# The second MLP's first product as seven products of halves, in units of 768 tokens, with w_out's parts read from DRAM

## The chip, the cores and the metric

The kernel runs on one core of a Trainium2 chip. The metric is the device time of one execution in microseconds (us). Before the change it is 1026.53 us, the median of three runs (1025.58 to 1028.79). All traces are profiles of one execution; times inside a trace count from the start of its span.

## The reference

Attention with a decay and a causal mask (4 sequences of 576 tokens, 8 heads of 64) gives x with 2304 tokens of 512 features. Two MLPs follow, one on the other's output:

```python
h = x @ w_in            # 512 -> 2048
r = np.maximum(h, 0.0)
x = (r * r) @ w_out     # 2048 -> 512
```

Everything is float32. The change is in the second of the two MLPs.

## The kernel before

A float32 matrix product is made of three products on the matrix engine (PE): each operand is cut into a high part, rounded to a shorter format that PE takes in one pass (fp32r), and a low part, the rest; high x high, high x low and low x high are added up in PSUM. A high part is a cast on ScalarE (ACT), a low part a subtraction on VectorE (DVE) or GpSimd (POOL).

The attention runs beside the first MLP (mlp_a), which goes over nine groups of 256 tokens. Sixteen tiles of the pool wp hold the first MLP's weights, one for each block of 128 hidden features: w_in's high and low part, then w_out's. The first MLP's output goes to y_d in DRAM. When its last group has used a weight tile for the last time, that tile takes the second MLP's weights of the same block. Those weights come from DRAM as 64-bit words; DVE takes three operations on 512 columns for each 512 KB (decode, L796 to L800), for 32 such words in all, w_in's and w_out's sixteen each.

The second MLP (mlp_b) goes over groups of 512 tokens: four, and a last one of 256. For each group the tokens are loaded from y_d and split (L983, L990, L993), alternately into a tile on the right (ysr) and one on the left (ysl) of SBUF. For each of 16 blocks PE makes the first product, 12 matmuls (4 blocks of the 512 inputs by 3 parts) into one of two banks hp (L841); ACT takes its positive part out of PSUM (L850), DVE multiplies that with the bank again (L853, the square), ACT casts it (L863) and POOL makes the low part (L866). The second product takes 12 matmuls of 512 columns, 3 for each 128 tokens, into four banks that hold the group's output (bk, L1015). After 16 blocks ACT and DVE evacuate them (L1025, L1027) and SP stores them.

The order of all instructions on an engine is fixed when the program is built: a planner plays the program through with its own costs and priorities (the first numbers in op(...)), and each engine then works through its list in order, waiting for semaphores. A list that waits holds up everything behind it. An operation given to either of two engines is placed by the planner. SP's list holds all DMAs.

## Time and profile before

| | us |
|---|---|
| median of the runs | 1026.53 |
| the profiled execution itself | 1022.93 |
| its span, first to last instruction | 1021.1 |
| PE busy | 995.2 |
| VectorE busy | 526.8 |
| ScalarE busy | 490.2 |
| GpSimd busy | 294.6 |
| DMA moved | 98.35 MB |

PE's granted clock is 90% or more of full speed in all but the second of the forty slices of the span, where the attention starts, and full in every stretch looked at from 100 us on. Busy times say how much an engine has to do. What an engine waits for, and whether that matters, is read from the chain of waits, which goes back from the last instruction to what released each step.

### The profile page before, as it was taken

How to read it: one execution, taken by the hardware profiler on the slowest of the kernel's cores; microseconds unless marked ns; L12 is line 12 of the kernel's file. 1: busy time of each engine (PE TensorE's matmuls, PEld its weight loads, DVE VectorE, ACT ScalarE, POOL GpSimd, SP SyncE). 2: the span in 40 equal slices, each digit the busy share in tenths (PEclk: the TensorE clock that was granted, in tenths of full speed). 3: DMA queues.
4: the chain of work that ended last, by engine and by line, in shares of the span. 5: the costliest groups of instructions: out<-in, count | busy, mean ns of one | idle time of the engine just before them, and what ended most of it. 6: DMA issues, size and time to landing. Idle time of an engine off the chain costs nothing.

```text
span 1021.1 us, 17203 instructions
## 1 busy us (share of the span) xinstructions
PE 995.2 (97%) x6637; PEld 865.6 (85%) x6637; DVE 526.8 (52%) x1241; ACT 490.2 (48%) x1001; POOL 294.6 (29%) x286
## 2 busy tenths in 40 slices
PE   5999999999999999999999999999999999999998
PEld 3888898887888898888999998888888888888897
DVE  7998666676677767677377698412112211211111
ACT  3766667777677777676222364322223222222222
POOL 2111143433434434333232222222222222222222
PEclk9799999999999999999999999999999999999999
DMA  9776246665665666566456344101000100000010
GB/s 248 228 215 182 80 95 127 133 133 122 130 135 123 133 134 129 119 120 127 104 162 179 107 132 155 44 1 62 21 1 1 62 1 1 11 32 1 1 42 21
DMA packets 164418, 98.35 MB, mean 96 GB/s; under 512 B 133936, under 2 KB 146992, under 8 KB 164208
## 3 DMA queue, kind: packets, MB, share of 16 engines
q1 hardware_dynamic: 164336, 97.25, 38.3%
q8 instruction: 52, 0.85, 0.3%
q14 instruction: 30, 0.25, 0.1%
HBM read 59.91 MB, written 10.03 MB: 68 GB/s over the span
## 4 chain that ended last, share of the span: by engine, by line
PE 84%; DVE 6%; DMA 6%; ACT 1%; issue 1%; SPq 1%; POOL 0%; DVEq 0%; ACTq 0%; POOLq 0%
PE hp L841 35%; PE bk L1015 19%; PE yp L916 16%; PE bk L732 7%; PE bk L692 4%; DMA sa<-in_w_dram 3%; DMA st<-in_w_dram 2%; PE bk L565 1%; PE bk L605 1%; DVE tmp L798 1%; DVE tmp L800 1%; PE bk L607 1%; DMA qk<-aug_d 0%; DVE wb L798 0%; DVE wb L800 0%
## 5 line engine op out<-in xcount | busy, mean ns | idle before, releaser
L866 POOL TENSOR_TENSOR gt<-sq,gt 128x512 fp32r<-128x512 f32 (+1 forms) x152 | 191.7, 1261 | 514.1 <-ACT gt L863 488.1
L853 DVE SCALAR_TENSOR_TENSOR sq<-hp,sq 128x512 f32<-128x512 f32 (+1 forms) x144 | 95.1, 661 | 332.8 <-ACT sq L850 332.5
L916 PE MATMUL yp<-gt,w 128*128 128x256 f32 x1728 | 232.5, 284 | 2.2 <-POOL gt L866 1.5
L841 PE MATMUL hp<-xk,w 128*128 128x256 f32 x1728 | 229.8, 285 | 0.0
L916 PEld LDWEIGHTS yp<-gt,w 128*128 128x128 f32 x1728 | 219.5, 191 | 4.4 <-POOL gt L866 2.1
L841 PEld LDWEIGHTS hp<-xk,w 128*128 128x128 f32 x1728 | 217.9, 192 | 0.5
L1015 PE MATMUL bk<-w,gt 128*128 128x512 f32 x864 | 209.8, 391 | 0.0
L850 ACT ACTIVATE sq<-hp 128x512 f32<-128x512 f32 (+1 forms) x152 | 87.4, 575 | 234.6 <-PE hp L841 201.5
L1015 PEld LDWEIGHTS bk<-w,gt 128*128 128x128 f32 x864 | 161.0, 188 | 34.3
L863 ACT CAST gt<-sq 128x512 fp32r<-128x512 f32 (+1 forms) x152 | 90.8, 598 | 158.1 <-PE bk L1015 109.8
L841 PE MATMUL hp<-ysr,w 128*128 128x512 f32 (+1 forms) x576 | 120.6, 358 | 0.0
L841 PEld LDWEIGHTS hp<-ysr,w 128*128 128x128 f32 x576 | 97.2, 188 | 18.4
L404 ACT ACTIVATE pp<-pp,stat 128x448 f32<-128x448 f32 (+1 forms) x128 | 78.3, 612 | 38.9 <-DVE stat L396 27.4
L841 PE MATMUL hp<-ysl,w 128*128 128x512 f32 x384 | 91.9, 389 | 0.0
L426 DVE SCALAR_TENSOR_TENSOR ph<-pp,stat,ph 128x320 f16<-128x320 f32 (+2 forms) x96 | 71.8, 751 | 27.8 <-ACT ph L419 26.7
L841 PEld LDWEIGHTS hp<-ysl,w 128*128 128x128 f32 x384 | 72.1, 188 | 14.9
L396 DVE CUSTOM_DVE_ANT_0 pp<-bk,mask 128x448 f32<-128x448 f32 (+1 forms) x128 | 59.3, 473 | 39.5 <-PE bk L692 38.8
L732 PE MATMUL bk<-pt,vv 64*128 64x64 f16 (+7 forms) x672 | 77.7, 253 | 0.0
L732 PEld LDWEIGHTS <-vv 128*128 128x128 bf16 (+3 forms) x672 | 37.0, 101 | 38.8 <-issue 24.9
L419 ACT ACTIVATE ph<-pp,stat 128x320 f16<-128x320 f32 (+2 forms) x96 | 63.6, 664 | 10.7 <-DVE stat L413 8.6
L435 POOL TENSOR_TENSOR vv<-vv 128x320 f32<-128x320 f32 x64 | 51.8, 809 | 55.7 <-DMA vv<-in_v_dram 51.1
L647 POOL TENSOR_TENSOR qk<-raw,qk 64x384 fp32r<-64x384 f32 x32 | 33.4, 1043 | 92.2 <-ACT qk L638 90.3
(132 smaller groups left out, 781.7 us busy)
## 6 DMA issues: line engine op xcount, KB each, us to landing
st<-in_w_dram SPq DMA_DIRECT2D x20, 512.0 KB
raw<-in_qk_dram SPq DMA_DIRECT2D x32, 288.0 KB
sa<-in_w_dram SPq DMA_DIRECT2D x18, 512.0 KB
X<-in_w_dram SPq DMA_DIRECT2D x14, 512.0 KB
vv<-in_v_dram SPq DMA_DIRECT2D x32, 160.0 KB
out_dram<-st SPq DMA_DIRECT2D x18, 256.0 KB
yf<-y_d SPq DMA_DIRECT2D x4, 1024.0 KB
raw<-in_w_dram SPq DMA_DIRECT2D x6, 512.0 KB
```

Of the source, the lines that this page charges most:

```text
L396: nc.vector.tensor_tensor_reduce(out=x[:rows, c0:c0 + wd], in0=src, in1=msk, scale=-0.125, scalar=3.0e38 if first else nmax[:rows, 5:6], o ...
L404: nc.scalar.activation(out=x, in_=x, func=AF.Exp, scale=-1.0, bias=nmax[:rows, t:t + 1], accum_out=ssum[:rows, t:t + 1])
L419: nc.scalar.activation(out=a, in_=x, func=AF.Copy, scale=r)
L426: nc.vector.scalar_tensor_tensor(out=flat[:rows, z:z + wd], in0=x, scalar=r, in1=flat[:rows, 128 * blk:128 * blk + wd], op0=ALU.mult, op1= ...
L732: nc.tensor.matmul(dst.rearrange("p (n c) -> p n c", n=rh.shape[1]), lhsT=lt, rhs=rh, start=(i == 0), stop=(i == len(todo) - 1), skip_grou ...
L841: nc.tensor.matmul(ps, lhsT=lt, rhs=rh, start=(k_ == 0 and c == 0), stop=(k_ == KD - 1 and c == 2))
L850: nc.scalar.activation(out=sq()[:, :c], in_=ps()[:, :c], func=AF.Relu)
L853: nc.vector.scalar_tensor_tensor(out=sq()[:, :c], in0=ps()[:, :c], scalar=0.0, in1=sq()[:, :c], op0=ALU.max, op1=ALU.mult)
L863: nc.scalar.copy(out=gt[0]()[:, :c], in_=sq()[:, :c])
L866: eng.tensor_tensor(out=gt[1]()[:, :c], in0=sq()[:, :c], in1=f32(gt[0]()[:, :c]), op=ALU.subtract)
L916: nc.tensor.matmul(yp[d // 2]()[:, d % 2], lhsT=lt, rhs=rh, start=(i == 0 and c == 0 and d % 2 == 0), stop=(i == NF - 1 and c == 2), skip_ ...
L1015: nc.tensor.matmul(ob[c](), lhsT=lt[:, cs], rhs=rh, start=(i == 0 and z == 0), stop=(i == NF - 1 and z == 2))
```

## The change

The second MLP works on units of 768 tokens, three in all. Its first product multiplies w_in, a matrix of 512 by 2048, with the tokens, in pairs of blocks: block p and block p+8 of the hidden features, by two halves of the 512 inputs, by two halves of 384 tokens. Such a product of two 2 x 2 matrices of blocks is made by seven products of blocks instead of eight. Their left operands are l11, l12, l22 and four sums s1 to s4 of w_in's blocks, their right operands r11, r21, r22 and four sums t1 to t4 of the tokens' quarters; each is split into its high and low part. A product takes 6 matmuls of 384 columns (2 blocks of 128 inputs by 3 parts). The seven results are combined after the product: ACT copies the first out of PSUM, and DVE makes seven sums, each of a bank and a tile in SBUF, of which four are the pair's hidden features (in r). The square then multiplies r with itself, 768 columns at a time, and the cast and the low part are 768 columns wide too.

The left operands of pairs 1 to 5 (p from 0 to 4) go into nine of the sixteen weight tiles as the first MLP frees them, the right operands of a unit into six; the last tile holds two buffers for w_out. The operands of pairs 6 to 8 are prepared during the first unit, in tiles (far) that are opened when all else is prepared. w_out's high and low parts are made once and stored in DRAM (wo_d); each step reads two blocks of them back, 512 KB each, in all units. The second product has six banks, one for each 128 tokens of a unit, and its matmuls are planned between the products of the next pair.

In the diff, tiles move too (sq, gt and xk go to a pool that is closed when the first MLP is done). Decoding a word takes the same three operations as before.

```diff
+    TU, TH, NP = 3 * GA, 3 * GA // 2, NF // 2
+    NU, NC = NT // TU, TU // 128
...
+    def unit_runs(u):
+        if u < 2:
+            return [(TH * x, (2 * u + x) * S, TH) for x in range(2)]
+        return [(TH // 2 * b, b * S + TH, TH // 2) for b in range(B)]
...
+    LEFT = ("l22", "l11", "l12", "s1", "s2", "s3", "s4")
+    RIGHT = ("r11", "t2", "r21", "t3", "t1", "t4", "r22")
+    ORDER = tuple(zip(("l11", "s2", "l12", "s3", "s1", "l22", "s4"), RIGHT))
+    wo_d = dram.tile([NF, 128, 2, 512], F32R, name="wo_d")
+    NEAR = 5
...
+    SUM, STAGEX, LWX = Pool([xf[:, 0:1024]]), Pool([xf[:, 1024:2048], xf[:, 2048:3072]]), Pool([xf[:, 3072:4096]])
+    UT = Pool([None] * 3, True)
+    RB, GTB = Pool([None] * 2, True), Pool([None] * 3, True)
+    RW = Pool([None] * 2, True)
...
+    SLOTS = ("s0", "l0", "s1", "l1", "s2", "l2", "s3", "s4", "l3", "y0", "y1", "y2", "y3", "y4", "y5", "ring")
...
+    def w_out_parts(i, prio, deps):
+        word, part = Buf(WORD), Buf(PART)
+        o = words(i, 1, STAGE, word, prio, deps, [word])
+        o = op("ACT", act(512), lambda: nc.scalar.copy(out=part()[:, 0], in_=word()), prio, [o], [word, part])
+        o = either_vp(512, lambda e: e.tensor_tensor(out=part()[:, 1], in0=word(), in1=f32(part()[:, 0]), op=ALU.subtract), prio, [o], [word, part])
+        return op("SP", P.COPY[0], lambda: nc.sync.dma_start(out=f32(wo_d[i]), in_=f32(part())), prio, [o], [part], data=1.46)
...
+    def w_in_forms(p, stage, lw, prio, deps, late, free):
+        l, sm = Buf(lw), Buf(SUM)
+        os_ = [words(i, 0, stage, lambda h=h: l()[:, h * 512:h * 512 + 512], prio, deps, [l]) for h, i in enumerate((p + NP, p))]
...
+        e = None
+        for f, a, b, how in (("s1", "l21", "l22", ALU.add), ("s2", "s1", "l11", ALU.subtract), ("s3", "l11", "l21", ALU.subtract), ("s4", "l12", "s2", ALU.subtract)):
+            e = either_vp(256, lambda eng, f=f, a=a, b=b, how=how: eng.tensor_tensor(out=x(f), in0=x(a), in1=x(b), op=how),
+                          prio, os_ + [e] + late, [l, sm])
...
+            n = 256 * (k - j)
+            dep = [slot_op[SLOTS[at[LEFT[j]]]]] if p < NEAR else [free]
+            h = op("ACT", act(n), lambda parts=parts: parts(0), prio, (os_ if j < 3 else [e]) + dep, uses)
+            got += [h, either_vp(n, lambda eng, parts=parts: parts(1, eng), prio, [h], uses)]
+            j = k
+        return got
...
+        def total(f, a, b, deps):
+            return either_vp(TU, lambda eng: eng.tensor_tensor(out=src(f), in0=src(a), in1=src(b), op=ALU.subtract), 40.0, deps)
+        done = {"r11": split("r11", ld)}
...
+    def first_products(q, u, p, ys):
+        t0, t1 = Buf(UT), Buf(UT)
+        r0, r1 = Buf(RB), Buf(RB)
+        g1, g0 = Buf(GTB), Buf(GTB)
+        h0, h1 = slice(0, TH), slice(TH, TU)
+        prods, prev = [], {}
+        e0 = EL + 1000 + q
...
+        def add(o, a, b):
+            return lambda: nc.vector.tensor_tensor(out=o(), in0=a()[:, 0:TH], in1=b(), op=ALU.add)
...
+        steps = (
+            [("copy", t0, None, [t0])],
+            [("u2", t1, t0, [t0, t1])],
+            [("c11", cols(r0, h0), t0, [t0, r0])],
+            [("u3", t0, t1, [t0, t1])],
+            [("c22", cols(r1, h1), t0, [t0, r1]), ("u4", t1, t1, [t1])],
+            [("c21", cols(r1, h0), t0, [t0, r1])],
+            [("c12", cols(r0, h1), t1, [t1, r0])],
+        )
+        after = dict(u2=["copy"], c11=["copy"], u3=["u2", "c11"], c22=["u3"], u4=["u3"], c21=["u3"], c12=["u4"])
+        done = {}
+        for s_, (lf, rf) in enumerate(ORDER):
+            ps = Buf(HP)
+            def prod(ps=ps, lf=lf, s_=s_):
+                for k_ in range(2):
+                    (wh, wl), (xh, xl) = form(p, lf, k_), y_form(s_, k_)
+                    for c, (lt, rh) in enumerate(((wh, xh), (wh, xl), (wl, xh))):
+                        nc.tensor.matmul(ps()[:, 0:TH], lhsT=lt, rhs=rh, start=(k_ == 0 and c == 0), stop=(k_ == 1 and c == 2))
+            m = op("PE", 6 * mmr(TH), prod, MLP + 10000 + 100 * q + 10 * s_, forms_of[p] + ys[s_], [ps])
+            prods.append(m)
+            for name, o, b, uses in steps[s_]:
+                if b is None:
+                    done[name] = op("ACT", act(TH, True), lambda o=o, ps=ps: nc.scalar.copy(out=o(), in_=ps()[:, 0:TH]), e0, [m], [ps] + uses)
+                else:
+                    done[name] = op("DVE", dve(TH), add(o, ps, b), e0, [m] + [done[x] for x in after[name]] + (late_ops if name[0] == "c" else []), [ps] + uses)
+        ready = []
+        for r, g, deps in ((r1, g1, [done["c21"], done["c22"]]), (r0, g0, [done["c11"], done["c12"]])):
+            o = op("DVE", dvs(TU), lambda r=r: nc.vector.scalar_tensor_tensor(out=r(), in0=r(), scalar=0.0, in1=r(), op0=ALU.max, op1=ALU.mult), e0, deps, [r])
+            h = op("ACT", act(TU), lambda r=r, g=g: nc.scalar.copy(out=g()[:, 0], in_=r()), e0, [o], [r, g])
+            l = either_vp(TU, lambda e, r=r, g=g: e.tensor_tensor(out=g()[:, 1], in0=r(), in1=f32(g()[:, 0]), op=ALU.subtract), e0, [h], [r, g])
+            ready.append((g, l))
+        return prods, ready
+    def second_products(q, u, p, ready, ob, last):
...
+        for x, ((g, lo), i) in enumerate(zip(ready, (p + NP, p))):
+            rw = Buf(RW)
+            ld = op("SP", P.COPY[0], lambda rw=rw, i=i: nc.sync.dma_start(out=f32(rw()), in_=f32(wo_d[i])), EL + 1000 + q, [out_ready[i], slot_op["ring"]], [rw], data=1.46)
+            for c in range(NC):
+                def m2(c=c, rw=rw, g=g, x=x):
+                    for z, (a, b) in enumerate(((0, 0), (0, 1), (1, 0))):
+                        nc.tensor.matmul(bank(ob[c]), lhsT=g()[:, a, c * 128:(c + 1) * 128], rhs=rw()[:, b], start=(p == 0 and x == 0 and z == 0),
+                                         stop=(p == NP - 1 and x == 1 and z == 2))
+                last[c] = op("PE", 3 * mmr(DM), m2, MLP + 10000 + 100 * (q + 1) + 10 * (n // 2 + 1) + 5, [lo, ld, last[c]], [g, rw, ob[c]])
+                n += 1
+    def store_unit(u, last, ob, deps):
...
-        opened_words = op("POOL", 0.01, open_words, -1.0e7, all_att)
...
-        opened_first = op("POOL", 0.01, open_first, -1.0e7, first_words)
-        opened_second = op("POOL", 0.01, open_second, -1.0e7, second_words)
-        dep = [opened_first]
-        for g, (t0, n) in enumerate(GB):
-            dep = [mlp_b(g, dep + [y for x in range(NGA) if any(t0 < s + k and s < t0 + n for _, s, k in runs(x * GA, (x + 1) * GA)) for y in y_stored[x]])]
...
+        last_a = [m2_of[0, NGA - 1, i] for i in range(NF)]
+        slots(last_a)
+        opened_prep = op("POOL", 0.0, open_prep, -1.0e7, all_att)
+        prep, near = [], []
+        for p in range(NP):
+            if p < NEAR:
+                forms_of[p] = w_in_forms(p, STAGE, LW, 9000.0 + 100.0 * p, [opened_prep], x_read, None)
+                prep += forms_of[p]
+            for i in (p + NP, p):
+                out_ready[i] = w_out_parts(i, 9050.0 + 100.0 * p, [opened_prep])
+                prep.append(out_ready[i])
+        opened_far = op("POOL", 0.0, open_far, -1.0e7, prep)
+        late_ops.append(op("POOL", 0.0, open_late, -1.0e7, last_a + x_read))
+        gone, taken, far = [[] for _ in RIGHT], [], []
+        waiting, sums = None, []
+        for u in range(NU):
+            stored = [y for x in range(NGA) if any(t < s + k and s < t + n for _, s, k in runs(x * GA, (x + 1) * GA) for _, t, n in unit_runs(u))
+                      for y in y_stored[x]]
+            ys, taken = inputs(u, x_read + [opened_prep] + stored + sums + far, gone, taken)
+            sums = [y for x in ys for y in x] + taken
+            if u == 0:
+                for p in range(NEAR, NP):
+                    forms_of[p] = w_in_forms(p, STAGEX, LWX, 9000.0 + 100.0 * p, sums, [], opened_far)
+                    far += forms_of[p]
+            ob, last = accumulators(), [None] * NC
+            for p in range(NP):
+                prods, ready = first_products(u * NP + p, u, p, ys)
+                second_products(u * NP + p, u, p, ready, ob, last)
+            gone = [[x] for x in prods]
+            store_unit(u, last, ob, far)
```

The change leaves the order of every engine as it was up to the end of the attention. PE's order in the middle of a unit, before (hp is the first product's bank, bk the output's banks, w the weights, gt the squared hidden features; x12 is twelve matmuls):

```order
L841 MATMUL hp0_85<-ysr_6645,w_6587 128x512 x12
L1015 MATMUL bk0_81<-w_6554,gt0_75 128x512 x2
L1015 MATMUL bk0_81<-w_6554,gt1_76 128x512
L1015 MATMUL bk1_82<-w_6554,gt0_75 128x512 x2
L1015 MATMUL bk1_82<-w_6554,gt1_76 128x512
L1015 MATMUL bk2_83<-w_6554,gt0_75 128x512 x2
L1015 MATMUL bk2_83<-w_6554,gt1_76 128x512
L1015 MATMUL bk3_84<-w_6554,gt0_75 128x512 x2
L1015 MATMUL bk3_84<-w_6554,gt1_76 128x512
L841 MATMUL hp1_86<-ysr_6645,w_6620 128x512 x12
```

and after (yp are two more output banks, g the squared features of 768 tokens; both operands of the first product and w_out's buffer stand in tiles w):

```order
L1212 MATMUL hp1_89<-w_6827,w_6696 128x384 x6
L1212 MATMUL hp0_88<-w_6871,w_6729 128x384 x6
L1238 MATMUL bk0_84<-w_6985,g1_6991 128x512 x3
L1238 MATMUL bk1_85<-w_6985,g1_6991 128x512 x3
L1212 MATMUL hp1_89<-w_6886,w_6696 128x384 x6
L1238 MATMUL bk2_86<-w_6985,g1_6991 128x512 x3
L1238 MATMUL bk3_87<-w_6985,g1_6991 128x512 x3
L1212 MATMUL hp0_88<-w_6926,w_6729 128x384 x6
L1238 MATMUL yp0_90<-w_6985,g1_6991 128x512 x3
L1238 MATMUL yp1_91<-w_6985,g1_6991 128x512 x3
L1212 MATMUL hp1_89<-w_6937,w_6729 128x384 x6
L1238 MATMUL bk0_84<-w_6985,g2_6992 128x512 x3
```

One product of 12 matmuls and all groups of the second took turns before; now two products of 6 stand at the start of each step and then single ones with two groups between them.

DVE's order while the second MLP's weights are decoded, before (sq is the square, sa the two tiles that loads arrive in, wb a decoded word; DMAHW is a wait for a DMA):

```order
L853 SCALAR_TENSOR_TENSOR sq_74<-hp_86,sq_74 128x512 [waits Activation_49]
L796 TENSOR_SCALAR wb_5706<-sa_5709 128x512 [waits DMAHW4_49]
L798 SCALAR_TENSOR_TENSOR wb_5706<-sa_5709,wb_5706 128x512 [waits DVE_49]
L796 TENSOR_SCALAR wb_5707<-sa_5710 128x512 [waits DMAHW5_49]
L800 SCALAR_TENSOR_TENSOR wb_5706<-sa_5709,wb_5706 128x512 [waits DVE_49]
L798 SCALAR_TENSOR_TENSOR wb_5707<-sa_5710,wb_5707 128x512 [waits DVE_49]
L800 SCALAR_TENSOR_TENSOR wb_5707<-sa_5710,wb_5707 128x512 [waits DVE_49]
L853 SCALAR_TENSOR_TENSOR sq_73<-hp_85,sq_73 128x512 [waits Activation_49]
L853 SCALAR_TENSOR_TENSOR sq_74<-hp_86,sq_74 128x512 [waits Activation_49]
L796 TENSOR_SCALAR X<-X 128x512 [waits DMAHW6_49,Pool_49]
```

and after, at the start of the first unit (hp, the sums' bank; st_82, st_83 and u their tiles in SBUF; stage, where a load arrives, word and X, which take a decoded one):

```order
L1052 SCALAR_TENSOR_TENSOR word_5707<-stage_5705,word_5707 128x512
L1048 TENSOR_SCALAR word_5706<-stage_5704 128x512 [waits DMAHW6_49]
L1189 TENSOR_TENSOR r_6994<-hp_88,st_82 128x384 [waits DVE_49,PE_49]
L1189 TENSOR_TENSOR st_83<-hp_88,st_83 128x384
L1189 TENSOR_TENSOR r_6994<-hp_89,st_82 128x384 [waits PE_49]
L1223 SCALAR_TENSOR_TENSOR r_6994<-r_6994 128x768 [waits DVE_49]
L1189 TENSOR_TENSOR r_6993<-hp_88,st_83 128x384 [waits PE_49]
L1050 SCALAR_TENSOR_TENSOR word_5706<-stage_5704,word_5706 128x512
L1225 TENSOR_TENSOR g_6990<-r_6994,g_6990 128x768 [waits Activation_49]
L1223 SCALAR_TENSOR_TENSOR r_6993<-r_6993 128x768 [waits DVE_49]
L1189 TENSOR_TENSOR st_82<-hp_88,u 128x384 [waits PE_49,Activation_49]
L1189 TENSOR_TENSOR r_6994<-hp_89,u 128x384 [waits DVE_49,PE_49]
```

Decode operations that wait for a DMA now stand between the sums that free the two banks hp.

DVE's order at the end of the first unit's fifth step, after the change only (far is pair 6's operands):

```order
L1223 SCALAR_TENSOR_TENSOR r_6993<-r_6993 128x768 [waits DVE_49]
L1189 TENSOR_TENSOR r_6994<-hp_89,st_83 128x384 [waits PE_49]
L1223 SCALAR_TENSOR_TENSOR r_6994<-r_6994 128x768 [waits DVE_49]
L1101 TENSOR_TENSOR far_7363<-X,far_7363 128x3x256 [waits DMAHW6_49,Activation_49]
L1189 TENSOR_TENSOR st_82<-hp_89,u 128x384 [waits PE_49,Activation_49]
L1189 TENSOR_TENSOR r_6993<-hp_88,u 128x384 [waits PE_49,Pool_49]
L1048 TENSOR_SCALAR X<-X 128x512 [waits DMAHW0_49,DVE_49]
L1048 TENSOR_SCALAR X<-X 128x512
```

The low part of pair 6's first operands stands between the fifth step's last square and the sixth step's first sums.

## Rows read from the trace of the kernel before

**Rows 1.** Page: PE's busy time, share of the span, instructions

```profile
PE 995.2 (97%) x6637; PEld 865.6 (85%) x6637; DVE 526.8 (52%) x1241; ACT 490.2 (48%) x1001; POOL 294.6 (29%) x286
```

**Rows 2.** Chain of waits, end of the first MLP to the end: start, us, what

```profile
614.25 1.44 PE yp L916 x12
615.69 2.81 PE hp L841 x12
618.50 1.43 PE yp L916 x12
...
639.45 2.81 PE hp L841 x12
642.26 2.76 PE bk L1015 x12
...
736.25 2.72 PE hp L841 x12
738.97 2.72 PE bk L1015 x12
...
1010.63 6.82 PE bk L1015 x30
1017.45 0.02 issue
1017.48 0.69 DVE st L1027
```

**Rows 3.** Busy times by stretch: us, PE, PEld, DVE, ACT, POOL, PE clock, DMA

```profile
500.00:628.00 128.00, 126.02 (x1013) 123.83 (x1012) 96.99 (x141) 46.84 (x82) 32.26 (x24) 1.00 0.46 141
560.00:570.00 10.00, 8.25 (x67) 7.85 (x66) 4.35 (x7) 2.84 (x5) 3.30 (x3) 1.00 0.30 105
```

**Rows 4.** Groups by shape, POOL and ACT: count, busy us, mean ns, idle before

```profile
L866 POOL TENSOR_TENSOR gt<-sq,gt 128x512 fp32r<-128x512 f32 x136 | 179.8, 1322 | 481.8 <-ACT gt L863 455.8 <-issue 14.4 <-PE hp L841 8.4
...
L863 ACT CAST gt<-sq 128x512 fp32r<-128x512 f32 x136 | 84.3, 620 | 142.1 <-PE bk L1015 93.8 <-DVE sq L853 46.4 <-PE yp L916 0.8
L850 ACT ACTIVATE sq<-hp 128x512 f32<-128x512 f32 x136 | 81.3, 598 | 219.7 <-PE hp L841 201.5 <-POOL gt L866 17.5
...
L866 POOL TENSOR_TENSOR gt<-sq,gt 128x256 fp32r<-128x256 f32 x16 | 11.8, 738 | 32.4 <-ACT gt L863 32.4
...
L863 ACT CAST gt<-sq 128x256 fp32r<-128x256 f32 x16 | 6.5, 407 | 16.0 <-PE bk L1015 16.0
...
L850 ACT ACTIVATE sq<-hp 128x256 f32<-128x256 f32 x16 | 6.2, 385 | 14.9 <-POOL gt L866 14.9
```

**Rows 5.** Line of the square: min, median and max ns, first and last start

```profile
L853 DVE SCALAR_TENSOR_TENSOR sq<-hp,sq x144: 424/692/694, 126.2 to 1013.5; 128x512 f32<-128x512 f32 x128, 128x256 f32<-128x256 f32 x16
```

**Rows 6.** Timeline, PE and ACT near 799 us: start, us, engine, line

```profile
798.88 1.32 PE L1015 MATMUL bk<-w,gt 128*128 128x512 f32 x5
799.13 0.60 ACT L850 ACTIVATE sq<-hp 128x512 f32<-128x512 f32 x1 [2.48 <-PE hp L841]
```

**Rows 7.** Timeline, POOL and DVE near 551 us

```profile
551.30 1.29 POOL L866 TENSOR_TENSOR gt<-sq,gt 128x512 fp32r<-128x512 f32 x1 [3.14 <-ACT gt L863]
...
551.35 1.78 DVE L798 SCALAR_TENSOR_TENSOR wb<-sa,wb 128x512 uint32<-128x512 uint32 x1
```

**Rows 8.** Line of a decode operation: min, median and max ns, first and last start

```profile
L798 DVE SCALAR_TENSOR_TENSOR wb<-sa,wb x10: 678/692/1785, 531.9 to 563.9; 128x512 uint32<-128x512 uint32 x10
```

**Rows 9.** Waits of DVE, 500 to 630 us: total us, times, longest

```profile
DVE wb L796 <- DMA sa<-in_w_dram: 10.6, 8, 3.6
...
DVE wa L796 <- DMA sa<-in_w_dram: 4.0, 4, 1.8
```

**Rows 10.** Timeline, SP's load of the last 256 tokens, 512 KB

```profile
791.78 0.53 SPq L983 DMA_DIRECT2D yf<-y_d  x1
```

**Rows 11.** Busy times by stretch behind that load, DMA share and GB/s last

```profile
791.50:793.50 2.00, 2.00 (x10) 1.62 (x9) 0.25 (x1) 0.00 (x0) 1.41 (x1) 1.00 0.17 21
793.50:795.50 2.00, 2.00 (x10) 1.62 (x9) 0.69 (x1) 0.60 (x1) 0.00 (x0) 1.00 0.76 239
```

More of the change, by code (lines that the diff above doesn't have):

```diff
@@ L942, in mlp_a @@
         y_stored[g] = outs
-    GB = [(t0, min(512, NT - t0)) for t0 in range(0, NT, 512)]
-    YF, YS = Pool([None]), Pool([None, None])
-    NWA, NWB = 8, 11
-    SA, WA, WB = Pool([None] * 2), Pool([None] * NWA), Pool([None] * NWB)
-    right, left = ExitStack(), ExitStack()
-    def place(pools, n, shape, dt, name, pl):
-        for x, y in zip(pools.free, tiles(pl, n, shape, dt, name)):
+    TU, TH, NP = 3 * GA, 3 * GA // 2, NF // 2
+    NU, NC = NT // TU, TU // 128
+    assert (B, S) == (4, 3 * TH // 2)
@@ L955, in place, with open_prep @@
             assert x[2] is None
             x[2] = y
[L958 removed]
+    def open_prep():
         att_stack.close()
[L960 to L970 removed]
@@ new lines, in open_prep @@
+        keep = ctx.enter_context(tc.tile_pool(name="keep", bufs=1, side="left", reuse_waits="tile"))
+        two_t.append(keep.tile([128, 2, TH], F32, name="t2"))
+        place(UT, [x[:, 512:512 + TH] for x in st_] + [keep.tile([128, TH], F32, name="u")])
+        pl = prep_stack.enter_context(tc.tile_pool(name="prep", bufs=1, side="left", reuse_waits="tile"))
+        place(STAGE, tiles(pl, 2, [128, 1024], F32, "stage"))
+        place(WORD, tiles(pl, 2, [128, 512], F32, "word"))
+        place(PART, tiles(pl, 2, [128, 2, 512], F32R, "part"))
@@ new lines, in open_prep, with open_far, open_late @@
+        place(LW, tiles(pl, NEAR, [128, 1024], F32, "lw"))
+    def open_far():
+        prep_stack.close()
+        pl = ctx.enter_context(tc.tile_pool(name="far", bufs=1, side="left", reuse_waits="tile"))
+        for p, x in zip(range(NEAR, NP), tiles(pl, NP - NEAR, [128, 7, 512], F32R, "far")):
+            for j, f in enumerate(LEFT):
+                WB[p, f] = (x, j)
+    def open_late():
+        mid_stack.close()
+        pl = ctx.enter_context(tc.tile_pool(name="late", bufs=1, side="right", reuse_waits="tile"))
+        place(GTB, tiles(pl, 3, [128, 2, TU], F32R, "g"))
+        place(RB, tiles(pl, 2, [128, TU], F32, "r"))
@@ L1198, in attention_then_two_squared_relu_mlps @@
-        for i in range(NF):
-            stage, words, deps = places(2 * i)
-            before = len(decoded)
-            got = weights(1, i, 9000.0 + 100.0 * i, 9000.0 + 100.0 * i, deps, [m2_of[0, NGA - 1, i]], stage, words)
-            if words is WA:
-                first_words += got
-            if words is WB:
-                second_words += got
-            if stage is SA:
-                first_words += decoded[before:]
-        opened_first = op("POOL", 0.01, open_first, -1.0e7, first_words)
```

216 lines of the change are left out of this document (144 added, 72 removed).

## Prediction

> **What bounds the kernel now.** First the busy times [rows 1]: the matrix engine PE works 995.2 us of 1021.1, so a change pays only by what it takes off PE's own time, less the waits it brings. Then the chain of waits [rows 2]: from 614.25 us to the end it is nothing but PE, so the second MLP has no wait in it. It starts at 615.69 us and its last product ends at 1017.45: 401.76 us, in which three runs of the first MLP still stand (the row at 618.50 and two like it, 4.3 us together). The second MLP costs PE 397.5 us. The same rows give the price of a product: 12 with 256 columns take 1.44 us, 120.0 ns each; 12 with 512 columns take 2.72 us (226.7 ns) to 2.81 us (234 ns) for the first product and 2.72 to 2.76 us (226.7 to 230 ns) for the second. The two levels alternate with the token group; I can't say why, and keep both. Last, the stretch in which the second MLP's weights are decoded, 500 to 628 us [rows 3]: PE is busy 126.0 of 128.0 us, and 1.75 of the lost 2.0 us fall between 560 and 570 us.
>
> **What the change takes from PE.** A step of the new code is a pair of feature tiles with a unit of 768 tokens: 7 products of 6 matmuls with 384 columns, then 36 matmuls with 512 columns; 8 pairs by 3 units make 24 steps. No row has 384 columns. The bounds are 120.0 ns (256 columns, too low) and 234 ns (512 columns, too high); since the difference between these two rows is what the columns cost, I take the straight line, 173.3 ns from the lower level and 177 from the upper. A step is then 42 x 173.3 + 36 x 226.7 ns = 7.28 + 8.16 = 15.44 us, or 7.43 + 8.28 = 15.71 us at the upper level. 24 steps make 370.6 to 377.0 us, against 397.5: a gain of 20.5 to 26.9 us, and I take 23.5, as the old code stood between its levels too. Weight loads rise from 960 to 1008 for the first product; they run beside the matmuls, which follow each other at 120.0 ns where columns are few, so they bound nothing at 384.
>
> **What it adds beside PE, in a step.** Durations for 384 and 768 columns follow the line through 256 and 512 [rows 4, 5]: a VectorE sum that reads PSUM 0.56 us (0.424 and 0.694), a square of 768 columns 0.96, a ScalarE copy out of PSUM 0.49 (0.385 and 0.598), its cast of 768 0.83 (0.407 and 0.620), GpSimd's subtraction of 768 1.91 (0.738 and 1.322). VectorE then has 7 x 0.56 + 2 x 0.96 = 5.8 us in a step, ScalarE 0.49 + 2 x 0.83 = 2.2, GpSimd 3.8, all far under 15.4. What counts is whether each result is there when PE asks. Two banks take the seven products, so product s+2 must find product s read; between most products PE has two groups of the second product, 6 x 226.7 ns = 1.36 us. The tightest place is the end of a step. Counted from the end of the sixth product: its sum ends at 0.81 us (0.25 us for the signal [rows 6]), the square at 1.8, the cast at 2.65, GpSimd's subtraction at 4.7; PE asks for it at 5.84, after 1.36 + 1.04 + 1.36 + 1.04 + 1.04. So 1.1 us are left.
>
> The other half of the step has less, by the port that VectorE and GpSimd share. In the trace a VectorE operation on two operands in SBUF that mostly takes 0.69 us [rows 8] took 1.78 when it began 0.05 us after a GpSimd subtraction of 1.29 us, and ended 0.54 us after it [rows 7]. The old square reads one operand from PSUM, and none of the 144 took longer than 0.694 us [rows 5]; the new one reads both from SBUF, so it can be held. If it is held until 4.7 us, the second square ends at 5.67, its cast at 6.54 and the copy of the next step's first product, queued behind that cast on ScalarE, at 7.06; PE needs that bank at 7.2. So 0.1 us is left, where an unheld square would leave 1.5. I count 1 us for all steps, between 0 and the 12 of a rival below. The Trainium skill, "SBUF — State Buffer", section "Who interferes with whom", has this as a rule: a VectorE instruction with two SBUF inputs contends with a GpSimd instruction that reads SBUF, and the later one waits for the whole of the other; one with a single SBUF input does not. The trace's 1.78 us agrees; without the rule the sum would be 1 us better.
>
> **What it adds outside the steps.**
> - Decoding before the second MLP, 500 to 628 us. The old queue waited 14.6 us for 18 loads [rows 9], which PE felt as most of its 2.0 us. Now 21 loads go through the two stage tiles before the second MLP, with 9 stores of 512 KB between them. The 32 old low parts of 512 columns (22 us at 0.69, as in [rows 8]) give way to 20 sums of 256 (8.5 us at 0.42), low parts of 35 x 256 columns and of 9 x 512 (18 us), a third of these on GpSimd, while 11 of the 32 words are now decoded later: no more work than before. I take 1.5 us more for the longer queue, from -1 (no stall falls on PE) to +6.
> - The start. After the first MLP's last product PE has seven products with nothing between them (7 x 1.04 = 7.3 us), for which VectorE must do 8 sums (the last six in the order's rows), 2 squares, 3 decode operations and a subtraction: 8 x 0.56 + 2 x 0.96 + 1.8 + 0.96 = 9.1 us. Following them one by one, the sixth to eighth product start about 1 us late. The first w_out parts come from DRAM and are asked for when the first MLP frees the last weight tile: a load of that size, 512 KB, moves at 239 GB/s about 1.3 us after its issue [rows 10, 11], so in about 4 us, and PE needs them after 8. Hidden by those seven products; were it in the open it would cost 4. I take 1, from 0 to 8.
> - Pairs 6 to 8, prepared during the first unit. On VectorE the low parts of pair 6's first forms stand behind the second square of step 5 (the order's last rows); they end about 0.25 + 0.56 + 0.96 + 0.95 = 2.7 us after that step's last product, and PE wants them at 1.36: 1.35 us late, up to 3.3 if GpSimd holds the port. I take 3 us for the three pairs, from 0 to 9.
> - Eleven loads are decoded in the first unit, in the queue whose sums free the banks. What hides them is their lead: by the order, most loads are issued with five or more instructions that PE paces between issue and decode. I count nothing; if that cover fails, it is the slower rival.
> - Two changes of unit: 7 splits, 4 sums and 6 evacuations beside a step of 15.4 us with some 10 us of work on GpSimd and ScalarE each; 0.5 us each, 0 to 5 in all. The end: no next step covers the last subtraction, 4.7 us after the sixth product where PE asks at 3.8; 1 us, 0 to 2. The last evacuation and its store stay as they were (0.69 us, from 1017.48).
>
> Sum: 23.5 - (1 + 1.5 + 1 + 3 + 1 + 1) = 15.0 us. The profiled execution took 1022.9 us (its span and 1.8 around it), so it becomes 1007.9; the median of the runs, 1026.5, lies 3.6 above it and becomes 1011.5.
>
> **Rivals.**
> - *Nothing is lost.* Every wait finds cover, as in the old second MLP, and the upper gain holds: 1026.5 - 23.5 to 1026.5 - 26.9, about 1001. For it: PE is the chain for 400 us without a break [rows 2]. Against it: six places above in which I count a wait.
> - *The port paces the steps.* If GpSimd's subtraction takes 0.5 us longer than the line says, the held square, the cast and the copy move with it, and PE waits 0.4 to 0.5 us in each step: 24 x 0.5 = 12 instead of 1, so 1022.5. For it: 0.1 us of slack. Against: sums that read PSUM are not held, and where VectorE does a subtraction itself, nothing is. The Trainium skill's rule on the shared port ("SBUF — State Buffer") is what would bring this about.
> - *VectorE's queue pays for the loads* (slower). Each load has been waited for 14.6 / 18 = 0.81 us in order; in the first MLP two whole tiles of 2.9 us lie between PE and VectorE, in the new unit only two banks of 1.04 us. If PE pays all 32 loads, 26 us: 1011.5 + 26 - 1.5 = 1036. It turns slower once PE pays more than 15 us, 0.5 us for each load. Against: VectorE's waits for loads reached PE with 2.0 of 14.6 us.
> - *The columns don't count*: 384 cost as much as 512. Then 1008 x 226.7 ns = 228.5 us instead of 174.7, 54 us more: 1065. The 256-column rows speak against it.
>
> **How the numbers follow.** Forecast 0.68; nothing lost 0.12; port 0.11; queue 0.08; columns 0.01. Two versions can be told apart when they differ by over 0.3%, about 3 us. Faster takes the first two and a part of the third, where the time ends below 1023.4: 0.68 + 0.12 + 0.05 = 0.85; the rest of the third and the mild end of the fourth is the same, 0.07; slower 0.08. The likeliest case alone spans 1004 to 1019, by the two levels of PE (3.2 us either way) and the bounds of the start and of pairs 6 to 8. The range reaches up to the port case and leaves out the slow queue: 1003 to 1024.
>
> **What would show it.** Right: a product of 6 matmuls with 384 columns every 1.04 to 1.06 us, a full step of 15.4 to 15.8 us, PE idle under 12 us after 500 us, most of it in the first unit. Waits of PE for the copy of the first product would show the port; PE waiting for VectorE sums behind a decode that waits for DMA would show the queue. It is wrong if steps of the second and third unit, which prepare nothing, take over 16.2 us, or if the matmuls with 384 columns come slower than 180 ns.

## The result, and the profile after

The changed kernel takes 1016.61 us, the median of four runs (1014.59 to 1020.15); the kernel before took 1027.66 beside it. The ratio is 0.989, with a 95% interval of 0.984 to 0.994. On another chip seven runs gave 1019.93 us and 0.993 (0.991 to 0.996). It is faster, by 7 to 11 us where 15 were forecast. The profiled execution took 1017.8 us, 5.1 less than that of before; all comparisons with the rows of before are made with it.

The page of the changed kernel, PE's and the other engines' busy time; 13.9 us less on PE than in [rows 1], with 142 us more on VectorE:

```profile
PE 981.3 (97%) x6683; PEld 879.9 (87%) x6685; DVE 669.3 (66%) x1400; ACT 463.2 (46%) x919; POOL 338.5 (33%) x281
```

The chain of waits in the second MLP (start, us, what), beside [rows 2]:

```profile
655.01 2.09 PE hp L1212 x12
657.10 1.40 PE bk L1238 x6
658.50 1.07 PE hp L1212 x6
659.57 1.40 PE bk L1238 x6
660.97 1.05 PE hp L1212 x6
...
670.79 2.09 PE hp L1212 x12
...
686.57 2.09 PE hp L1212 x12
...
702.35 2.09 PE hp L1212 x12
```

A step begins with two products (x12): it takes 15.78 us, three times here and to 0.02 us in all steps from the second to the last but one, whether pairs are prepared in it, the unit changes or neither. A product of 384 columns takes 1.05 to 1.07 us, six matmuls of 512 columns 1.40 (233 ns).

Busy times by stretch (us, PE, PEld, DVE, ACT, POOL, PE clock, DMA share, GB/s), beside [rows 3]; the last row sums nine stretches of 40 us from 640 to 1000:

```profile
500.00:560.00 60.00, 57.34 (x472) 55.72 (x470) 39.12 (x58) 17.09 (x30) 18.51 (x13) 1.00 0.58 188
560.00:570.00 10.00, 9.98 (x70) 9.99 (x71) 6.87 (x11) 2.68 (x5) 4.42 (x3) 0.83 0.62 200
570.00:600.00 30.00, 27.94 (x219) 27.54 (x218) 15.99 (x22) 10.34 (x17) 9.76 (x9) 0.94 0.40 131
600.00:628.00 28.00, 28.00 (x231) 28.00 (x230) 23.64 (x31) 15.59 (x25) 13.92 (x10) 1.00 0.11 39
628.00:640.00 12.00, 9.96 (x62) 9.09 (x61) 11.86 (x16) 3.39 (x6) 6.16 (x4) 1.00 0.53 164
...
sum 360.00, PE 360.00 PEld 322.75 DVE 214.71 ACT 71.28 POOL 114.97; mean PE 40.00 PEld 35.86 DVE 23.86 ACT 7.92 POOL 12.77
```

From 640 to 1000 us PE waits for nothing. What is lost lies ahead: 4.74 us idle from 500 to 628 (before 1.98), 2.04 at the start of the second MLP, and two stretches in which the granted clock is below full. At 0.83 over 10 us and 0.94 over 30, PE ran some 7 us at 1.2 GHz instead of 2.4, which costs 3.5; in the profile of before, the clock stayed at 1.00 there. Each time PE had just stood still; but its stops of 0.9 us at 527 us and of 1.7 us at 633 us were not followed by a lower clock. Its waits and VectorE's (us in total, times, longest), beside [rows 9]:

```profile
PE yp L920 <- POOL gt L870: 3.6, 5, 1.2
PE hp L1212 <- DVE r L1189: 1.7, 1, 1.7
PE yp L920 <- ACT gt L867: 1.4, 2, 0.8
...
DVE lw L1048 <- DMA stage<-in_w_dram: 11.3, 7, 2.6
DVE word L1048 <- DMA stage<-in_w_dram: 9.7, 7, 2.6
```

VectorE waits 21.0 us for loads, 14.6 before. The first MLP's squares stand behind those waits, and PE waits for what ScalarE (gt L867) and GpSimd (gt L870) make of them.

The forms of the new work by shape, and after them the timeline of a step around its end, beside [rows 4, 5, 7]:

```profile
L1223 DVE SCALAR_TENSOR_TENSOR r<-r 128x768 f32<-128x768 f32 x48 | 75.4, 1571 | 1.5
L1225 POOL TENSOR_TENSOR g<-r,g 128x768 fp32r<-128x768 f32 x36 | 67.3, 1870 | 216.0 <-ACT g L1224 180.9 <-PE hp L1212 24.9 <-issue 10.2
L1224 ACT CAST g<-r 128x768 fp32r<-128x768 f32 x48 | 40.1, 836 | 188.9 <-DVE r L1223 188.7
L1189 DVE TENSOR_TENSOR r<-hp,st 128x384 f32<-128x384 f32 x64 | 35.6, 556 | 71.6 <-PE hp L1212 71.6
```

```profile
796.24 2.16 DVE L1223 SCALAR_TENSOR_TENSOR r<-r 128x768 f32<-128x768 f32 x1
...
796.85 2.25 PE L1212 MATMUL hp<-w 128*128 128x384 f32 x12
...
798.09 0.48 ACT L1218 COPY st<-hp 128x384 f32<-128x384 f32 x1 [2.44 <-PE hp L1212]
798.49 0.84 ACT L1224 CAST g<-r 128x768 fp32r<-128x768 f32 x1
...
809.56 0.96 DVE L1223 SCALAR_TENSOR_TENSOR r<-r 128x768 f32<-128x768 f32 x1
...
811.51 1.85 POOL L1225 TENSOR_TENSOR g<-r,g 128x768 fp32r<-128x768 f32 x1 [10.26 <-ACT g L1224]
812.02 2.15 DVE L1223 SCALAR_TENSOR_TENSOR r<-r 128x768 f32<-128x768 f32 x1
```

The first square of a step takes 0.96 us; the second, begun 0.51 us after GpSimd's subtraction, takes 2.15 and ends 0.81 us after it. It is held, and PE does not notice: ScalarE copies the next product out of its bank (798.09) ahead of the cast (798.49) that waits for such a square, the one begun at 796.24.

### The profile page after: what moved, and what is told of

Same layout as the page of the kernel before. It is cut to its first block, busy times and chain, and to the rows that moved or that the text cites. A ratio compares the mean times of both kernels' runs of the same rounds, so it can differ in the third digit from the quotient of the medians.

```text
span 1016.0 us, 17569 instructions
## 1 busy us (share of the span) xinstructions
PE 981.3 (97%) x6683; PEld 879.9 (87%) x6685; DVE 669.3 (66%) x1400; ACT 463.2 (46%) x919; POOL 338.5 (33%) x281
## 4 chain that ended last, share of the span: by engine, by line
PE 69%; DVE 10%; issue 8%; DMA 8%; POOL 3%; ACT 2%; SPq 1%; POOLq 0%; DVEq 0%; ACTq 0%
PE hp L845 14%; PE yp L920 13%; PE hp L1212 12%; PE bk L1238 10%; PE bk L736 7%; PE yp L1238 5%; PE bk L696 4%; DMA stage<-in_w_dram 4%; POOL g L1225 2%; DMA st<-in_w_dram 2%; DVE w L1101 1%; PE bk L609 1%; PE bk L569 1%; DVE tmp L802 1%; DVE lw L1052 1%
## 5 line engine op out<-in xcount | busy, mean ns | idle before, releaser
L870 POOL TENSOR_TENSOR gt<-sq,gt 128x512 fp32r<-128x512 f32 x72 | 97.4, 1352 | 175.0 <-ACT gt L867 158.8
L1238 PE MATMUL bk<-w,g 128*128 128x512 f32 x576 | 149.5, 396 | 0.2 <-POOL g L1225 0.2
L1225 POOL TENSOR_TENSOR g<-r,g 128x768 fp32r<-128x768 f32 x36 | 67.3, 1870 | 216.0 <-ACT g L1224 180.9
L1212 PE MATMUL hp<-w 128*128 128x384 f32 x630 | 124.7, 337 | 1.8 <-DVE r L1189 1.7
L1238 PEld LDWEIGHTS bk<-w,g 128*128 128x128 f32 x576 | 107.3, 188 | 18.8 <-POOL g L1225 0.6
L1212 PEld LDWEIGHTS hp<-w 128*128 128x128 f32 x630 | 112.2, 188 | 9.5 <-issue 2.0
L1223 DVE SCALAR_TENSOR_TENSOR r<-r 128x768 f32<-128x768 f32 x48 | 75.4, 1571 | 1.5
L1212 PE MATMUL hp<-w,far 128*128 128x384 f32 x378 | 75.2, 337 | 0.0
L1238 PE MATMUL yp<-w,g 128*128 128x512 f32 x288 | 75.0, 395 | 0.0
L1212 PEld LDWEIGHTS hp<-w,far 128*128 128x128 f32 x378 | 67.7, 188 | 4.8
```

The lines of the kernel that those rows point to most:

```text
L870: eng.tensor_tensor(out=gt[1]()[:, :c], in0=sq()[:, :c], in1=f32(gt[0]()[:, :c]), op=ALU.subtract)
L1212: nc.tensor.matmul(ps()[:, 0:TH], lhsT=lt, rhs=rh, start=(k_ == 0 and c == 0), stop=(k_ == 1 and c == 2))
L1223: o = op("DVE", dvs(TU), lambda r=r: nc.vector.scalar_tensor_tensor(out=r(), in0=r(), scalar=0.0, in1=r(), op0=ALU.max, op1=ALU.mult), e0, ...
L1225: l = either_vp(TU, lambda e, r=r, g=g: e.tensor_tensor(out=g()[:, 1], in0=r(), in1=f32(g()[:, 0]), op=ALU.subtract), e0, [h], [r, g])
L1238: nc.tensor.matmul(bank(ob[c]), lhsT=g()[:, a, c * 128:(c + 1) * 128], rhs=rw()[:, b], start=(p == 0 and x == 0 and z == 0), stop=(p == NP ...
```

## The experiments

Kernels e1 to e4 ran on one chip, e5 to e8 on another, e9 on its own, e10 to e12 on a third; each set has runs of the kernel before beside it (1026.4 to 1028.7 us). Durations of single matmuls are worked out from the starts of successive ones in the traces.

**e1, e2, e3: does the place of g in SBUF set the 233 ns?** In the built programs all tiles on the right side of SBUF start 32 bytes beyond a multiple of 64. One line moves them; e2 has 16 instead of 8 numbers, e3 is the same line in the kernel before.

```diff
+    ctx.enter_context(tc.tile_pool(name="pad", bufs=1, side="right")).tile([128, 8], F32, name="pad")
```

> The changed kernel with every tile on the right side of SBUF moved down by 32 bytes, so that the tiles g of the squared features, which PE loads as weights in the second product, start at a multiple of 64 bytes in a partition; nothing else differs. Theory (place): a PE operand that starts 32 bytes beyond a multiple of 64 costs some ns per matmul, and that is the upper of the two levels of before. Then 512 columns take 226.7 ns instead of 233, 384 columns 173.3 instead of 176, a step 15.44 us instead of 15.78, and the time falls by 24 x 0.34 = 8 us to about 1008.5 us. Rival (traffic): the level comes from what else uses SBUF beside PE (the stores of w_out's parts, VectorE, GpSimd), or from both operands lying on the same side. Then the step stays at 15.78 us and the time at 1016.6.

> The control: the same tiles moved down by 64 bytes, so that they still start 32 bytes beyond a multiple of 64. Place: step 15.78 us and 1016.6 us, as in the changed kernel. If any move of the tiles against each other mattered, the step would differ from 15.78 us.

> The kernel before with its right side moved down by 32 bytes, so that the tokens' tile ysr starts at a multiple of 64 bytes as ysl does. Place: the first product of the groups of 512 tokens on the right falls from 2.81 us to 2.72 and the second from 2.76 to 2.72; 0.13 us in each of 32 blocks of two groups is 4 us, 1027.7 - 4 = about 1023.5 us. The group of 256 tokens, also on the right, stays at 1.44 us. Rival (traffic, or the side on which the tile lies): both levels stay, 1027.7 us.

e1: 1014.24 us (ratio 0.988, 0.985 to 0.991), e2: 1009.12 (0.984, 0.981 to 0.988), e3: 1023.91 (0.997, 0.994 to 0.999). The steps of e1 and e2 take 15.80 us. The theory of 64 bytes falls: g starts on such a multiple in e1 and its matmuls still take 233.3 ns. But e3 fits the rival no better. The chain of waits of e3 where the group on the right ends and one on the left begins (start, us, what):

```profile
703.21 2.76 PE hp L842 x12
705.97 2.77 PE bk L1016 x12
708.74 2.72 PE hp L842 x12
711.46 2.72 PE bk L1016 x12
```

The first product fell from 2.81 to 2.76 us, not to 2.72. And in e1 and e2 the first MLP's matmuls of 256 columns, which read xk and gt on that side, took 117.3 to 118.1 ns in the middle of the attention instead of 120. So the place counts, by another rule. e2 was meant as a control and lies 7 us below the first runs of the changed kernel; its steps are no shorter, so the time comes from ahead of the second MLP.

**e4: late decodes.** No work differs, only what the planner takes a transfer to cost.

```diff
-        o = op("SP", P.COPY[0], load, prio, deps, [st], data=1.46 if wide else 0.73)
+        o = op("SP", P.COPY[0], load, prio, deps, [st], data=2.19 if wide else 0.73)
...
-        return op("SP", P.COPY[0], lambda: nc.sync.dma_start(out=f32(wo_d[i]), in_=f32(part())), prio, [o], [part], data=1.46)
+        return op("SP", P.COPY[0], lambda: nc.sync.dma_start(out=f32(wo_d[i]), in_=f32(part())), prio, [o], [part], data=2.19)
```

> The changed kernel with the planner told that a load or store of 512 KB in the decoding takes 2.19 us on the DMA (512 KB at the 239 GB/s of the trace) instead of 1.46; no work differs, only the order that it writes. Theory (late decodes): in the stretch of 500 to 628 us PE is idle 4.7 us, because the first MLP's squares stand behind decodes that wait for loads, and each such stop is followed by 3.4 us at the lower clock (1.2 GHz). With later decodes PE's idle time there falls under 2.5 us, at most one dip of the clock stays, and the time falls by 2 to 6 us to 1011 to 1014.5. Rival (bandwidth): the loads and stores themselves are too slow for the stretch; VectorE's wait moves to another place, PE is idle as long, or longer at the start of the second MLP, and the time stays at 1016.6 within 1.5 us or rises.

1012.43 us (ratio 0.986, 0.983 to 0.989). Its busy times by stretch and VectorE's waits for loads:

```profile
500.00:560.00 60.00, 60.00 (x502) 59.62 (x499) 46.88 (x61) 17.74 (x31) 17.03 (x12) 1.00 0.54 183
560.00:600.00 40.00, 40.00 (x335) 40.00 (x335) 28.62 (x39) 16.84 (x27) 13.92 (x12) 1.00 0.37 119
600.00:628.00 28.00, 25.69 (x194) 24.92 (x192) 26.61 (x35) 13.30 (x20) 12.62 (x8) 1.00 0.30 95
```

```profile
DVE word L1048 <- DMA stage<-in_w_dram: 0.8, 2, 0.4
DVE lw L1048 <- DMA stage<-in_w_dram: 0.5, 1, 0.5
```

The waits fell from 21.0 us to 1.3, PE is not idle once between 500 and 600 us, and the clock stays at 1.00. The same loads and stores fit: it was the order. About 2.3 us come back at 600 to 628, where the second MLP starts. Its gain in time can't be read here, since the changed kernel itself was not on this chip; e11 is for that.

**e5, e6: is it the height?** Both change one word, the side of the pool base.

```diff
-    base = ctx.enter_context(tc.tile_pool(name="base", bufs=1))
+    base = ctx.enter_context(tc.tile_pool(name="base", bufs=1, side="right"))
```

> The changed kernel with X and st moved from the left to the top end of SBUF's right side, which moves g and far down by 24,576 bytes: g (weights of the second product) lies at 180,192 to 198,624 instead of 204,768 to 223,200, and everything else that PE reads in the second MLP below it; no work and no order differs. New theory (height), after alignment fell: PE's reads of tiles far up in a partition are slower. Before, the matmuls that read ysr (212,960 and up) took 234 ns and those of ysl (181,376 to 197,760) 226.7. Then the second product falls from 233 to 226.7 ns and the first from 176 to 173.3, a step from 15.78 to 15.44 us, and the time by 8 us against the changed kernel on the same chip. Rival (fixed): the longer time belongs to the pattern of the steps (short groups of six, or both operands of the first product in tiles of one pool), wherever the tiles lie: 15.78 us, no difference.

> The kernel before with its base tiles (X, xk, sq, gt, st) moved to the top of SBUF: gt, the weights of the second product, from 164,992 to 212,960, while ysr comes down from 212,960 to 163,808. Height: the first product takes 2.72 to 2.76 us for 12 matmuls in all groups of 512 tokens, on the right too, and the second product 2.80 us in all of them, on the left too, where both took 2.72. Rival (the side or the group): groups on ysr stay at 2.81 and 2.76, groups on ysl at 2.72. The time: 32 blocks by 0.08 us more and 32 by about 0.03 less, +1 to +3 us, 1028 to 1030.

e5: 1017.70 us (0.991, 0.989 to 0.994), steps of 15.78: no difference. e6: 1030.29 us (1.005, 1.003 to 1.007). Its chain of waits, again from a group on ysr to one on ysl:

```profile
706.43 2.81 PE hp L841 x12
709.24 2.81 PE bk L1015 x12
712.05 2.73 PE hp L841 x12
714.78 2.81 PE bk L1015 x12
```

Height falls: ysr came down and stays slow. But the second product, 2.72 us with ysl before, is now slow with both, since gt was moved. What ysr, the moved gt and g share is the distance of their starts from a multiple of 512 bytes, counted from the weight tiles w: 352. The tiles that gave 226.7 ns for 512 columns had 0; for 256 columns 0 and 352 both gave 120.0. Since w starts at the same place in all runs, the distance from w can't be told from the place itself; what follows counts from w.

**e7: the changed kernel again.**

> The changed kernel itself once more, as it is, beside the others on the same chip: 1016.6 us if its four runs stood for it; 1009 to 1014 if the 1009.1 us of the kernel that was only moved by 64 bytes stands for it. With clock dips that come at other places, PE's idle time in 500 to 628 us should again be 4 to 7 us.

1019.93 us (0.993, 0.991 to 0.996). PE is idle 6.0 us from 500 to 628, as expected, and the granted clock is 0.91 from 560 to 600, as the rows of the first trace give it too. e2's 1009 us did not stand for this kernel.

**e8: eight products.**

```diff
-                for k_ in range(2):
+                ks = (0, 1, 0, 1) if s_ == 0 else (0, 1)
+                for n_, k_ in enumerate(ks):
```

> The changed kernel with the six matmuls of each step's first product done twice into the same bank (so the first product is counted double in what is computed): PE does eight products in a step instead of seven, as the plain product of halves would need, and all else stays. Theory (PE alone sets the step): a step grows by 6 x 174.5 ns = 1.05 us to 16.83, the time by 24 x 1.05 = 25 us, to 1037 to 1041 us, slower than before by 10 to 15 us: the gain is the left-out product and nothing else. Rival (some of the step is a wait for GpSimd, ScalarE or VectorE that the longer product hides): less than 20 us more.

1041.10 us (1.015, 1.012 to 1.018), 21.2 us above e7 on the same chip, where the runs of each spread by 6 us. A step begins with three products (x18) in its chain of waits:

```profile
709.66 3.13 PE hp L1213 x18
...
726.48 3.13 PE hp L1213 x18
```

It takes 16.82 us, 1.04 more, which is 25.0 in 24. The steps follow PE alone to 0.01 us. With eight products, units of 768 tokens and w_out from DRAM would lose.

**e9: ten distances in one run.** Pads between the buffers, as below for g, and other starts within the tiles of the tokens' operands.

```diff
-        place(GTB, tiles(pl, 3, [128, 2, TU], F32R, "g"))
+        place(GTB, padded(pl, (64, 64, 128), 3, [128, 2, TU], F32R, "g"))
```

> The changed kernel with pads of 32 to 128 bytes between tiles, nothing else: each buffer that PE reads starts at another distance from a multiple of 512 bytes, counted from the weight tiles w. Distances: in the first MLP gt 32, 64, 128 and 192, xk 256, 320 and 352 (changed kernel: 352 for all, kernel before: 0); in the second product g 64, 128 and 256 (352; before 0); in the first product the tokens' operands 192, 32, 64, 128, 256, 96 and a mixture (0). Theory (distance): what a matmul costs beyond its columns depends on the distance between the operand that streams and the weights that are loaded meanwhile. It explains what stands so far: distance 0 gave exactly 120.0 and 226.7 ns, 352 gave 120.0 and 233, 320 gave 117.5 and 233, and the level followed neither the side, nor the height, nor a multiple of 64. Then each distance shows its own duration in each product of every step, and some lie under 120.0, 173.3 and 226.7 ns. Rival (pattern): the durations stay at 120, 174 to 176 and 233 whatever the distance. The time: within 8 us of the changed kernel's 1016 to 1020, either way.

1015.17 us (two runs). Means, and medians for 256 columns, whose intervals hold waits:

| operand, columns | distance: ns |
|---|---|
| g loaded, 512 | 64: 232.9; 128: 231.9; 256: 230.5 (352: 233.4 in the changed kernel) |
| gt streamed, 256 | 32: 118; 64: 117; 128: 120; 192: 117 |
| xk streamed, 256 | 256: 118; 320: 118; 352: 119 |
| tokens streamed, 384 (the same product of the step in the changed kernel, at 0) | 192: 174.1 (174.0); 32: 175.3 (173.8); 64: 173.9 (177.2); 128: 175.6 (174.4); 256: 177.6 (177.7); 96: 176.5 (174.4) |

Steps take 15.69, 15.70 and 15.75 us in turn, with a period of three as the three buffers g rotate. So the distance counts, and the pattern alone does not set the level; but its worth is 1 to 3% and its order is not one I could have guessed. The row of the tokens tells little: each distance stands at another product of the step, and those alone differ by 4 ns at distance 0.

**e10, e11, e12: the distances put right.** Pads at the end of the pools late and mid (e10), with them e4's change and two more output buffers (e11), one pad of 352 bytes in the kernel before (e12).

```diff
+        pl.tile([128, 88], F32, name="pad_g")
...
+    mid.tile([128, 8], F32, name="pad_x")
```

> The changed kernel with two pads and nothing else: g starts at a distance of 0 from a multiple of 512 bytes, counted from the weight tiles (352 in the changed kernel, 0 for gt in the kernel before), and xk and gt of the first MLP at 320 (352; the runs with 320 and 288 took 117.5 ns for 256 columns instead of 120). Theory (distance): with all operands of the second MLP at distance 0 its second product takes 226.7 ns instead of 233 and a step 15.78 - 36 x 0.0067 = 15.54 us, or 15.44 if the first product falls to 173.3 ns with it: 5.8 to 8 us. The first MLP gives 2 us more. In all 1008 to 1012 us. Rival (pattern): the second product stays over 230 ns, since distance 256 only brought 230.3; then 1014 to 1018.

> The kernel of the run above, and with it the planner's 2.19 us for each load and store of the decoding, and two more output buffers for the last unit (the last evacuation in the changed kernel waited 1.79 us for a store, of which about 0.9 us were lost). Theory: the late decodes cost the changed kernel 6 us or so between 530 and 590 us (54 us for 192 matmuls of the first MLP's second product, where the kernel before took 48 and the run with the planned loads 46); their gain is the same beside the pads: PE idle under 1 us in 500 to 600 us, no dip of the clock there, and the time 5 to 8 us below the run above on the same chip, 1001 to 1006 us. Rival (chip): the planned loads were not faster than the kernel moved by 64 bytes on their chip (1012.4 and 1009.1 us), so the order is worth nothing, and only the 0.9 us of the end come.

> The kernel before with its tile ysr at distance 0 like ysl. Distance: the first product of all groups takes 2.72 us and the second too, 32 x 0.13 = 4 us less than before, 1022 to 1024 us; against it the run above e11 shows what the change is worth when neither kernel pays for the places of its tiles. Rival: 2.76 us stays, as with 64 bytes.

e10: 1009.98 us (0.986, 0.982 to 0.990). e11: 1004.41 (0.980, 0.977 to 0.983). e12: 1022.94 (0.997, 0.994 to 0.999). The chains of waits of e12, on ysr, and of e10:

```profile
640.14 2.72 PE hp L842 x12
642.86 2.72 PE bk L1016 x12
```

```profile
694.93 2.08 PE hp L1214 x12
697.01 1.39 PE bk L1240 x6
698.40 1.04 PE hp L1214 x6
...
710.57 2.08 PE hp L1214 x12
```

In the kernel before, distance 0 removes the upper level wholly (2.81 and 2.76 to 2.72 us). In the changed one a step falls to 15.64 us: the first product is at 174.0 ns on the mean, but the second at 231.5. For that the rival was right, though the time lies where the theory put it. Why the second misses 226.7 I can't say: its matmuls come in sixes here and in twelves in the kernel before, and no run changes that. e11 beside e10 shows what e4 was worth on one chip, 5.6 us by the medians. Its busy times by stretch:

```profile
500.00:560.00 60.00, 60.00 (x510) 59.81 (x509) 46.48 (x62) 17.82 (x30) 17.10 (x12) 1.00 0.54 185
560.00:600.00 40.00, 39.85 (x338) 39.64 (x338) 30.92 (x41) 17.71 (x28) 15.49 (x12) 1.00 0.33 108
600.00:628.00 28.00, 24.37 (x179) 23.35 (x178) 26.59 (x37) 12.27 (x19) 12.65 (x8) 1.00 0.41 124
```

PE is idle 0.15 us in 500 to 600, against 6.8 in e10, and 3.6 against 1.8 after. The output buffers brought nothing: the span ends 5.2 us after PE's last product, as in e10. e11 beats both kernels, and is 18.5 us faster than e12, in which the old second MLP has its best places too (e11's 117.5 ns for 256 columns in the first MLP is a part of that).

## Why the prediction was right, and where it was not

The direction, the range and the mechanism held: PE's own time sets the second MLP, seven products make it shorter (e8), and the losses lie outside the steps. The sum was 5 us too good by the medians (1011.5 and 1016.6) and 10 by the profiled executions (1007.9 and 1017.8). By its terms, in us of the profiled execution:

| term | forecast | measured |
|---|---|---|
| PE's gain in 24 steps | 23.5 | 397.5 - 24 x 15.78 = 18.8 |
| steps and port | -1 | 0 |
| decoding, 500 to 628 | -1.5 | 2.76 idle + 3.5 by the clock = -6.3 |
| start | -1 | -2.0 |
| pairs 6 to 8 | -3 | 0 |
| unit changes | -1 | 0 |
| the end | -1 | -1.4 |
| ahead of 501 us | none | -2.3 |
| sum | 15.0 | 6.8 |

The execution gained 5.1 us, 1.7 less. Most of this lies in the stops: the profile's modelled ends of matmuls reach into them, and from start to start PE's stops from 501 to 640 us cost 8.6 us after and 2.6 before, where its idle time says 6.8 and 2.0. The last row but one is no part of the change, which leaves all orders as they were up to there: PE reached the same matmul of the first MLP at 501.2 us instead of 498.9, but in the traces of e3 and e12, which are the kernel before up to there, at 502.1 and 504.2. So that profile of before was an early one. Three terms that came to nothing (5 us) made up for half of what the first, the decoding and the start cost beyond the forecast (10.5 us): that the median came within 5 us is in part luck. Of the signs of being right, the step and PE's idle time (6.9 us after 500 us) came as said, but most of that idle time lies ahead of the first unit, not in it.

- *PE's gain* is the step that failed in size, below its lower bound of 20.5. The 384 columns came as the straight line had them (175.6 ns, between 173.3 and 177). The second product did not: I took 226.7 to 230 ns from the old second product, as if its level belonged to it, and it took 233. I had noted that the level alternates with the token group and left it unexplained; the tile on which it turns stands in the timeline by its name (ysl, ysr), and where the new code puts g could have been compared with it. e12 shows that in the old kernel the place of ysr is the whole of the two levels; e10 gives back 3.4 of the 4.7 us missing.
- *Decoding* failed too, just past the end of its range (6). I costed the longer queue and PE's share of it, but not what follows a stop: PE runs at half its clock for some us. That made 3.5 us of 6.3, though not every time: in the traces of e6 and e12, the old kernel, one such stretch of 3.4 us falls at 530 and 532 us, in those of before and e3 none. The cause was as named, VectorE's list waiting for loads; e4 and e11 show that the order alone brings it about and can take it away.
- *Pairs 6 to 8* were mis-placed by a step, by the order's last rows as I read them. The low parts of pair 6's first forms do stand behind a square, but that of the fourth step: the fifth begins at 686.4. The tile's rows (min, median, max ns, first and last start) show VectorE at it from 687.9 to 691.1 us, and PE taking the tile first at 702.2, with the sixth step:

```profile
L1212 PE MATMUL hp<-w,far x378: 334/337/346, 702.2 to 1000.4; 128*128 128x384 f32 x189
...
L1101 DVE TENSOR_TENSOR far<-X,far x2: 1212/2185/3158, 687.9 to 719.6; 128x768 fp32r<-128x768 f32 x1, 128x1024 fp32r<-128x1024 f32 x1
```

- *The port*, priced at 1, cost the steps nothing. The square is held, as the Trainium skill, "SBUF — State Buffer", section "Who interferes with whom", has it: the trace agrees, 2.15 us against 0.96. My 0.1 us of slack rested on the copy standing behind the cast on ScalarE; it stands ahead of it.
- *The start* lost 1.7 of its 2.0 us at the fifth product, which waits for a sum that stands on VectorE behind two low parts of the tokens' operands, a decode operation and an evacuation. Those two low parts stand in the timeline beside two subtractions on GpSimd:

```profile
628.94 4.32 POOL L1146 TENSOR_TENSOR w<-X,w 128x768 fp32r<-128x768 f32 x2 [0.32 <-ACT w L1144]
...
629.82 3.85 DVE L1146 TENSOR_TENSOR w<-X,w 128x384 fp32r<-128x384 f32 x2
```

  The two took 3.85 us together, where the four later ones of that size took 0.55 each. So the port, which I priced in the steps, was the likelier cause of this wait; no run tests it apart. Past it the rival of *VectorE's queue* did not come true: from 640 us on the loads were hidden, as their lead said.
- *The end*: the wait of PE that I priced was 0.2 us; the rest lies behind its last product (5.05 us to the end of the span, 3.7 before). It did not grow by the wait for an output buffer, as I thought after the first trace; e11 shows that. Eight stores that SP issues one by one (0.55 to 0.66 us each), instead of two, are the likelier reason, which no run tested.

## What to carry to other kernels

When one kind of matmul shows two levels of duration in a trace, find out which tile the level follows before using either for new code; a pad of some bytes may be worth per cents of a matmul's time. Where decodes and loads share an engine's list with the work that feeds PE, give the planner the transfer time that the trace shows, since a short stop of PE can cost some us at the lower clock besides its idle time. Count the steps in an order by the tiles' numbers, not by the look of the rows.
